# A fused DeltaNet and MLP kernel: another written-out order of its instructions behind entry 380

## The chip, the cores and the metric

The kernel runs on one core of a Trainium2 chip. The time is the device time of one execution in microseconds (us); the median of several executions counts. A profiled execution has a span as well, from its first to its last instruction. Five engines work beside each other, each through its own list of instructions in order: TensorE (PE, with its weight loads as PEld), VectorE (DVE), ScalarE (ACT), GpSimd (POOL) and SyncE (SP), which only issues transfers. ACT and POOL can issue transfers too.

## The reference

The first half is a delta rule over time, for 4 batches x 8 heads, 768 steps and a head size of 48, from a state of zeros (k_n is k divided by its norm plus 1e-6):

```python
for t in range(S):
    y[:, :, t] = np.einsum('bhd,bhde->bhe', q[:, :, t], state)
    v_old = np.einsum('bhde,bhd->bhe', state, kt)
    state = state + bt[:, :, :, None] * np.einsum('bhd,bhe->bhde', kt, vt - v_old)
```

The second half takes the 3072 rows of y (8 heads x 48 = 384 wide) through a two-layer network with a tanh GELU: `h = x @ w_in` (384 to 2048), `g = gelu(h)`, `out = g @ w_out` (2048 to 384). Inputs and output are float32.

## The kernel before

Time is cut into 12 chunks of 64 steps. A chunk c has two units, u = 2c and 2c + 1, of 16 (batch, head) pairs each, two of them stacked on the 128 partitions. All matmuls take bf16.

For a unit, `prep` (L470) makes bf16 copies of k and q and a scaled k (`kc`, `kb`, `qb`), turns them on their side (a transposing transfer `turn` on SP for most units), multiplies them into two masked 64x64 matrices per head (`G2` to `ln` and `G` to `wp`, both masked on DVE, L534), and then inverts a triangular 64x64 matrix per head in five rounds. Round i is a relay between engines: 8 matmuls `Ai` on PE (L575), an addition `rti` on DVE (L587; the tile is rt in rounds 1 to 3 and rl in rounds 4 and 5), 8 matmuls `Bi` on PE, and an eviction of the result from PSUM into the block-diagonal tile bd, from which the next round reads. Round 1 begins with `X1`, which fills bd from ln, mostly on POOL.

The eviction has three forms, and the order picks one for each unit and round. `bde` copies the two 64x512 halves apart (L332). `bdf` copies the lower half apart and brings the upper one as a 128x512 product with a column of zeros and ones (L338). `xi` copies all of it densely as one 128x512 (L332), after which two copies `bdc` (L617) spread it from SBUF into bd, on POOL or DVE.

For a chunk, `chain` (L620) carries the state on: `K` (state times keys), `R` on DVE (L660), `U` (the inverse times R, L670), its eviction `Un`, the state's growth `S` and `Sn` on DVE (L689), and the output of the chunk, `Q` and `O` (L647, L695), evicted by `On` and turned by `X` or by a transfer `turnx`. `mlp` (L716) then runs 48 matmuls of 128x256 in 16 groups `up` (L724), four GELUs on ACT (L728), 32 matmuls of 128x384 in 8 groups `down` (L735), evictions `Z0`, `Z1` and the transfers `out`.

What runs when is no loop: the string ORDER names every operation once, with the engine behind a colon where there is a choice and the PSUM bank behind an @. `order` (L154) makes the lists of the engines from it, and `emit` (L192) adds the waits that the data and the banks need. So an engine never passes a waiting instruction, and a transfer issued from ACT stands in ACT's list between its evictions. Two ways through a step (`A`, `rt` or `J`, `C`, `rj`; `nsq` or `nsa`) are picked by naming one of them.

```python
                for waits, o in plan[ename]:
                    for n, v in waits.items():
                        e.wait_ge(sems[n], v)
                    ins = o.fn(e, tile)
```

Of the kernel before, what the change touches and what calls it, by code (L numbers as in the profile page):

```python
# [16 lines left out]
ORDER = """  # L17
beta01:a one pad1 k0x1.11:a k0x0.01:a bdz0:g upone1 wz:d fill23@0 fill20@1 fill46@0 fill16@1 fill63@4 fill26@1 half:d fill25@0 fill12@2
fill54@5 ident pad3:g k0x0.10 tmplz:d tmpl0 k0x1.00:a k0x1.10:a k0x1.01:a mmup:d pad0 mmlo:d mlo0 fill64@0 k0x0.00 mlo1 tmpl1 two:d triln1:d
triwpm3:d triwpm1:d ladj16:d fill37@1 identf k0x0.11 ident2 ladj32:d fill28@4 sq.0a:d fill65@3 mup0 k1.00 fill56@4 sum.0a triln0:d fill41@1  # L20
fill52@6 beta00 betaT0@3 betaN000 betaN001 betaN010 betaN011 k1.01 epsb k1.10:a fill45@2 beta11:a k1.11 fill22@1 beta10 sq.0b:g tabS pow.0a
eps.0a twob:d J1.1@3 sum.0b q0.1 mup1 nsa.0a v0.11 inv.0a ib.0a upone0 v0.10 pow.0b fill55@2 q0.0:a eps.0b nsa.0b sq.1:d fill36@0 kb.0 kc.1
bdz1:g k2.10 fill49@2 inv.0b ib.0b:g kb.1:g betaT1@0 kc.0 Tc.1@1 fill9@2 betaA111 betaA110 betaA101 sum.1 pow.1 eps.1:g nsq.1:g kTc.1 q1.1
fill60@4 Tb.0@2 kTb.0 Tc.0@4 kTc.0 Tb.1@1 inv.1 triwpm0:d betaA100 ib.1 GM.0@6 ln.0 kb.3:g v1.11:a v0.01 X11.0 wpm.0 kTb.1:a GM.1@4 ln.1
X10.0 v0.00:a qb.0:a Tq.0@1 wpm.1 kc.3 Tk.3@2 triln3 A1.0@0 X10.1:d kTq.0 GQ.0@4 k2.00:a kTk.3:a q1.0:a X11.1 C1.1 rj1.1 rt1.0 B1.0@0 k2.01
pad2 kb.2 wpq.0 bde10.0 kc.2:d GM.3@6 ln.3 B1.1@1 bde10.1:d bde11.0 A2.0@0 rt2.0 bde11.1 A2.1@1 rt2.1 Tk.2@3 triwpm2 B2.0@2 B2.1@0 qb.1:a
v1.00 Tq.1@1 v1.10 v1.01 wpm.3 bde21.0:d k2.11 sq.2 sum.2 bde20.0 A3.0@2 fill1@4 fill4@5 fill42@4 fill14@5 q2.0 bdf20.1 bdf21.1:d A3.1@0
rt3.0 B3.0@2 kTk.2:a GM.2@4 rt3.1 triln2 ln.2 w2.1 qb.2:a bdz4:g bdz3:g X10.3 kTq.1:a X11.3 w1.1 A1.3@0 pad5:g pow.2 B3.1@1 k3.10 GQ.1@6
wpm.2 rt1.3 kc.5 k4.10 q2.1 bdf30.0 bdf31.0 A4.0@2 rt4.0 vs.1 B1.3@0 R0b.0:g bdf30.1 bdf31.1 A4.1@1 bdz2:g wpq.1 v2.00 bdf10.3 qb.3:g
eps.2:g B4.0@2 bde41.0 nsq.2:g bde40.0 X11.2 rt4.1 q3.0 X10.2 A1.2@4 rt1.2 B4.1@1 bde41.1:d w1.0 bde40.1 Tq.2@3 kTq.2 B1.2@4 bde10.2  # L30
triwpm4:g A5.0@5 rt5.0 A5.1@1 rt5.1 bde11.2 bdf11.3:d k3.01 B5.0@2 bde50.0 A2.2@3 rt2.2 B5.1@4 bde50.1:d bde51.0 k3.00 bde51.1 B2.2@0
bde21.2 bde20.2 inv.2 A2.3@1 rt2.3 R0a.0:g U.0@4 Un.0:d B2.3@1 A3.2@0 rt3.2 q4.0 Tq.3@2 O.0@4 On.0:d fill6@3 bde21.3 qb.5:g B3.2@0 bde20.3
A3.3@1 rt3.3 kTq.3:a GQ.3@6 X.0@2 xT.0:d B3.3@1 triwpm5:g bdf30.2 bdf31.2 A4.2@0 rt4.2 bdf30.3 bdf31.3:d up4.0@2 up12.0@4 up13.0 k3.11 wpq.3
ib.2:g kb.5:g B4.2@0 up5.0 up6.0 up7.0 up14.0 A4.3@1 up15.0 up0.0@6 q3.1 tabG bde41.2:d bde40.2 up1.0 up2.0 A5.2@0 rt4.3 gelu1.0 pad4:g
kb.4:g kc.7 up3.0 B4.3@1 w2.0 kc.4:g sq.3:g sum.3 k4.00 k5.10 q4.1 gelu3.0 gelu0.0 qb.4:g T.4@2 kT.4:a T.5@4 rt5.2 bde41.3:d bde40.3:d kT.5
pow.3 eps.3:g up8.0@6 up9.0 v2.11 A5.3@0 rt5.3 k5.00:a G2.5@2 ln.5 bdz5:g kc.6:g X11.5 k4.01:a G2.4@4 S.0@0 Sn.0 ln.4 X11.4 X10.4 G.4@2 wp.4
up10.0 qb.9:a up11.0 gelu2.0 nsq.3:g qb.6:g qb.7:g k4.11 K.1@0 R.1 inv.3 ib.3:g kb.6:g kb.7:g v3.11 G.5@4 wp.5 B5.2@2 sq.4 down10.0@3 A1.4@1
down00.0@0 bde51.2 rt1.4 kc.8 down01.0 X10.5 sum.4 pow.4 eps.4:g B5.3@4 bdf50.3 B1.4@1 bde10.4 k5.01 bde11.4:d down11.0 A1.5@5 rt1.5
down02.0 k5.11 sq.5:g kc.10:g A2.4@1 v4.10 v4.11 rt2.4 turn.7 v2.10 bdf51.3 bde50.2 B1.5@4 bde10.5:d bde11.5 down03.0 Z0.0 B2.4@2 v3.10
bde21.4:d kc.9:g U.1@6 Un.1 A2.5@5 rt2.5 q5.0 down12.0 GQ.2@0 wpq.2 Q.1@6 bde20.4 A3.4@2 turn.6 v3.00:a rt3.4 G2.7@4 O.1 On.1 S.1@0 Sn.1  # L40
nsq.4:g down13.0 inv.4 ib.4:g X.1@2 B2.5@6 xT.1:d kb.9:g v4.01 sum.5 pow.5 eps.5:g kb.8:g Z1.0 bde20.5 B3.4@7 bdf30.4 turn.9 fill47@3 v3.01
ln.7 bdf31.4 v2.01:a up0.1@0 up1.1 up2.1 up3.1 bde21.5:d gelu0.1 q6.1 A4.4@2 rt4.4 qb.8:a up8.1@4 up9.1 k7.00 A3.5@3 rt3.5 B4.4@2 bde41.4
k7.11 G2.6@0 ln.6 G.7@6 wp.7 q7.0 up10.1 B3.5@3 bde31.5 bde30.5 X10.6 up11.1 gelu2.1 up4.1@0 up5.1 up6.1 G.6@6 bde40.4:d A4.5@3 k6.10:a
up7.1 down10.1@2 wp.6 k7.10 rt4.5 A5.4@4 rt5.4 up12.1@6 out11.0 gelu1.1 X11.6 A1.6@5 X11.7 X10.7 A1.7@3 rt1.7 rt1.6 k7.01 turn.8 B4.5@4
bdf40.5 q6.0 up13.1 B5.4@0 up14.1 xi5.4:d bdf41.5 B1.7@3 bdf10.7 bdc50.4 up15.1 B1.6@1 bdc51.4 bde10.6:d bde11.6 out00.0 vs.2 A5.5@5
down11.1 down12.1 q7.1 rt5.5 bdf11.7:d B5.5@5 nsa.5 gelu3.1 xi5.5 bdc50.5 A2.6@4 rt2.6 sq.7 Q.2@0 K.2@6 R.2 bdc51.5 A2.7@3 rt2.7 k6.00:a
B2.6@4 xi2.6:d bdc21.6 down00.1@5 U.2@6 Un.2 down01.1 B2.7@3 inv.5 sum.7 bde20.7:d fill27@4 O.2 bdc20.6 q5.1 G2.8@6 ln.8 A3.6@4 X10.8 ib.5:g
bde21.7 A3.7@3 rt3.7 On.2 X11.8 turnx.2 v4.00:a down13.1 Z1.1 rt3.6 G.8@6 wp.8 k6.01 vs.3 k6.11 B3.7@0 bde31.7 bde30.7 S.2@2 Sn.2 kb.10:g
B3.6@4 kb.11:g down02.1 bde30.6 A1.8@6 rt1.8 down03.1 bde31.6 kc.11:g qb.11:g Z0.1 out00.1 out11.1 A4.7@0 rt4.7 A4.6@2 B1.8@3 bdf10.8
bdf11.8 G.9@4 G2.9@6 ln.9 up4.2@0 up5.2 up6.2 B4.7@3 up7.2 up0.2@6 up1.2 up2.2 k8.10:a wp.9 rt4.6 up8.2@4 B4.6@2 bde41.6:d X11.9 bdf40.7  # L50
bdf41.7 gelu1.2 up9.2 up10.2 up11.2 up3.2 A2.8@3 qb.12:a up12.2@0 bde40.6:d A5.6@2 qb.10:g rt5.6 gelu2.2 gelu0.2 up13.2 A5.7@4 rt5.7 up14.2
rt2.8 B5.6@2 xi5.6 X10.9 A1.9@5 rt1.9 pow.7 sq.6:g B5.7@4 xi5.7 turn.10 sum.6 bdc50.7 up15.2 gelu3.2 down00.2@3 B2.8@2 bde21.8 bde20.8:d
k8.01 B1.9@4 bde10.9 K.3@6 R.3 G2.10@0 down10.2@5 q8.1 q8.0 turn.11 A3.8@2 rt3.8 kc.13:g eps.7:g bdc50.6 bdc51.6 down01.2 bdc51.7 U.3@6
ln.10 X10.10:d X11.10 bde11.9 A2.9@2 B3.8@4 Q.3@0 rt2.9 v5.00 Un.3 O.3 On.3 turnx.3 G.10@6 pow.6 eps.6:g B2.9@2 bdf20.9 bdf21.9 bde30.8:d
down11.2 down02.2 down03.2 Z0.2 wp.10 A1.10@6 v6.11 rt1.10 A3.9@1 rt3.9 kc.12 qb.13:g k8.00 bde31.8 down12.2 k8.11 qb.15:a nsq.6:g inv.6
ib.6:g S.3@2 kb.12:g turn.12 Sn.3 down13.2 Z1.2 kb.13:g nsa.7 A4.8@0 B3.9@1 bdf30.9 rt4.8 G2.11@6 ln.11 G.11@2 wp.11 B4.8@0 bde40.8:d
# [742 lines left out]
```

## Time and profile before

| | |
|---|---|
| time, median of 3 runs | 264.47 us (260.86 to 264.93) |
| span of the profiled execution | 258.8 us |
| the profiled execution's own time | not given apart; the nearest of the three runs, 260.86 us, is 2.1 us over the span |
| PE busy | 242.1 us, 94% of the span |
| DVE busy | 209.5 us, 81% |
| ACT busy | 185.1 us, 72% |
| POOL busy | 136.2 us, 53% |

A busy share says that an instruction was in flight, from its issue to its result. For PE, whose matmuls overlap, it hides short stops between two matmuls; for the others it is nearer to the time that the instructions take. What bounds a stretch is read from the stretch. Entry 380 of the order, where the change begins, is reached at 47.6 us of the span or a little later.

### The profile page before, as it was taken

The page shows a single profiled execution, that of the slowest core. Times are in us where ns is not written, and L with a number is a line of the kernel's source. Part 1 is how long each engine was busy: PE and PEld are TensorE (multiplying, and loading weights), DVE is VectorE, ACT ScalarE, POOL GpSimd, SP SyncE. Part 2 cuts the span into 40 slices and gives each one's busy share as a digit, 9 for nine tenths or more (in the row PEclk, how much of TensorE's full clock was granted, in tenths as well). Part 3 has the DMA queues.
Part 4 walks back from the last instruction along what each step waited for, and adds up shares of the span by engine and source line. Part 5 has one row for each costly group of instructions (what it writes and reads, how often), then busy time and mean ns, then how long its engine had stood idle before and what let it go on. Part 6 is the DMA issues. An engine that isn't in the chain of part 4 may idle for free.

```text
span 258.8 us, 12244 instructions
## 1 busy us (share of the span) xinstructions
PE 242.1 (94%) x5490; PEld 189.6 (73%) x5490; DVE 209.5 (81%) x358; ACT 185.1 (72%) x295; POOL 136.2 (53%) x198
## 2 busy tenths in 40 slices
...
GB/s 88 200 191 182 212 185 200 135 132 151 164 198 146 167 107 134 159 102 165 160 47 157 155 96 185 53 74 123 155 66 106 128 48 4 3 5 124 30 63 61
DMA packets 116788, 31.46 MB, mean 122 GB/s; under 512 B 110848, under 2 KB 115968, under 8 KB 116736
## 3 DMA queue, kind: packets, MB, share of 16 engines
...
q8 instruction: 43, 0.70, 1.1%
...
## 4 chain that ended last, share of the span: by engine, by line
PE 81%; DVE 8%; POOL 4%; issue 3%; ACTq 2%; ACT 1%; POOLq 0%
PE ps L724 24%; PE ps L735 24%; PE ps L575 20%; PE ps L530 4%; PE ps L647 3%; PE ps L670 2%; PE ps L695 2%; ACTq L432 2%; DVE rt L587 1%; PE ps L682 1%; DVE wp L534 1%; POOL nrm L458 1%; DVE ln L534 1%; PE ps L394 1%; POOL bd L564 1%
## 5 line engine op out<-in xcount | busy, mean ns | idle before, releaser
L332 ACT ACTIVATE bd<-ps 64x512 bf16<-64x512 f32 x127 | 72.8, 587 | 20.5 <-PE ps L575 18.7
L724 PE MATMUL ps<-xT,W 128*128 128x256 bf16 x576 | 76.3, 273 | 0.7 <-issue 0.7
L735 PE MATMUL ps<-W,gT 128*128 128x384 bf16 x384 | 73.8, 326 | 0.0
L728 ACT ACTIVATE gT<-ps 128x1024 bf16<-128x1024 f32 x48 | 48.5, 1020 | 15.1 <-PE ps L724 14.7
L724 PEld LDWEIGHTS ps<-xT,W 128*128 128x128 bf16 x576 | 50.7, 98 | 7.2 <-issue 1.0
L587 DVE TENSOR_TENSOR rt<-ps,two 128x512 bf16<-128x512 f32 x71 | 47.6, 683 | 5.4 <-PE ps L575 4.9
L735 PEld LDWEIGHTS ps<-W,gT 128*128 128x128 bf16 x384 | 33.0, 97 | 16.9 <-ACT gT L728 0.2
L564 POOL TENSOR_SCALAR_AFFINE_SELECT bd<-ln 64x512 bf16<-64x512 bf16 x44 | 29.1, 664 | 24.5 <-DVE ln L534 20.9
L332 DVE CAST bd<-ps 64x512 bf16<-64x512 f32 x51 | 34.8, 686 | 5.2 <-PE ps L575 4.2
L534 DVE CAST_PREDICATED wp<-mup,ps 128x1024 bf16<-128x1024 uint16 (+1 forms) x28 | 29.7, 1062 | 1.5 <-PE ps L530 1.4
L575 PE MATMUL ps<-rt,bd 128*128 128x64 bf16 x576 | 28.5, 195 | 2.0 <-DVE rt L587 1.5
L458 POOL TENSOR_TENSOR nrm<-nrm,half 128x16 f32<-128x16 f32 x9 | 26.2, 2908 | 7.6 <-DVE nrm L456 7.4
L617 POOL COPY bd<-xi 64x256 f32<-64x256 f32 x27 | 10.8, 404 | 34.6 <-DVE xi L332 19.5
L575 PE MATMUL ps<-wp,bd 128*128 128x64 bf16 (+1 forms) x576 | 27.1, 189 | 1.5 <-POOL bd L564 1.0
L575 PEld LDWEIGHTS ps<-rt,bd 128*128 128x128 bf16 x576 | 23.5, 99 | 6.7 <-DVE rt L587 2.4
L575 PEld LDWEIGHTS ps<-wp,bd 128*128 128x128 bf16 x576 | 23.0, 98 | 6.2 <-POOL bd L564 1.5
L587 DVE TENSOR_TENSOR rl<-ps,two 128x384 bf16<-128x384 f32 (+1 forms) x48 | 23.0, 484 | 4.8 <-PE ps L575 4.4
L575 PE MATMUL ps<-ln,bd 128*128 128x48 bf16 (+1 forms) x384 | 18.8, 190 | 2.8 <-issue 1.6
L575 PE MATMUL ps<-rl,bd 128*128 128x64 bf16 x384 | 18.8, 193 | 0.7 <-DVE rl L587 0.7
L575 PEld LDWEIGHTS ps<-ln,bd 128*128 128x128 bf16 x384 | 15.5, 98 | 5.2 <-issue 1.8
L575 PEld LDWEIGHTS ps<-rl,bd 128*128 128x128 bf16 x384 | 15.7, 98 | 3.0 <-DVE rl L587 1.1
L485 POOL TENSOR_TENSOR tok<-kraw,nrm 128x384 bf16<-128x384 f32 x19 | 15.6, 829 | 4.2 <-PE ps L682 2.7
...
## 6 DMA issues: line engine op xcount, KB each, us to landing
qraw<-in_q_dram SPq DMA_DIRECT2D x21, 192.0 KB, 5.0
out_dram<-ob SPq DMA_DIRECT2D x21, 192.0 KB, 3.4
...
W<-in_moe_w_in_dram POOLq DMA_DIRECT2D x2, 768.0 KB, 10.1
...
```

The source lines that it names most:

```text
L332: return e.activation(out, in_, ACT.Copy) if e is nc.scalar else e.tensor_copy(out, in_)
L458: if e is nc.scalar else e.tensor_tensor(nr[:, 1, hx], nr[:, 0, hx], half[:, hx], ALU.pow), reads=[nrn, "half"] + ["one", "roots"] * (c < ...
L485: A(("dve", "pool"), op("kb"), lambda e, P: e.tensor_tensor(kb, kr, nr[:, 5, hx].unsqueeze(2).to_broadcast(full), ALU.mult), reads=[f"kraw ...
L530: ins = e.matmul(o, kT[s][r, y, g, hf(a)], src)
L534: return e.copy_predicated(out.rearrange("p (x g) t -> p x g t", x=2), mask[:, 0:wd].bitcast(U16).unsqueeze(1).unsqueeze(1).to_broadcast([ ...
L564: A(("pool", "dve"), op(f"X1{a}"), lambda e, P, src=ln[m][hf(a), :, :], dst=bd[b_][hf(a), :, hf(a)], a=a: e.affine_select(out=dst, in_=src ...
L575: ins = e.matmul(P(name)[:, C * h + cs.start:C * h + cs.stop], bd[b_][:, h, :], rhs[:, h, cs], **kw)
L587: A(("dve",), op(f"rt{i}"), lambda e, P, i=i, cs=cs, cn=cn, r_=r_: e.tensor_tensor(r_[:, :, cs], P(ps(f"A{i}")).rearrange("p (h t) -> p h ...
L617: A(("pool", "dve"), op(f"bdc{i}{a}"), lambda e, P, src=xi[i_][hf(a), :, :], dst=bd[b_][hf(a), :, hf(a)]: e.tensor_copy(dst.bitcast(F32), ...
L724: ins = e.matmul(P(ph)[:, 256 * f:256 * f + 256].rearrange("p (x t) -> p x t", x=2), W1[:, j, 128 * (i + f):128 * (i + f) + 128], x_[:, :, ...
L728: A(("act",), f"gelu{i // 4}.{c}", lambda e, P, i=i, ph=ph: e.activation(g_[:, i:i + 4, :], P(ph).rearrange("p (f t) -> p f t", f=4), ACT. ...
L735: ins = e.matmul(P(po)[:, 0:DM], g_[:, f, 128 * b:128 * b + 128], W2[:, f, :], start=(f == 0), stop=(f == FC - 1))
```

## The change

Only the string ORDER is replaced, and with it the file is 7 lines shorter: a line L332 of before is L325 of after, and so on. The first 380 entries name the same operations on the same engines. Behind them the order is new throughout; a line of it on each side:

```diff
-up10.0 qb.9:a up11.0 gelu2.0 nsq.3:g qb.6:g qb.7:g k4.11 K.1@0 R.1 inv.3 ib.3:g kb.6:g kb.7:g v3.11 G.5@4 wp.5 B5.2@2 sq.4 down10.0@3 A1.4@1
...
-rt2.8 B5.6@2 xi5.6 X10.9 A1.9@5 rt1.9 pow.7 sq.6:g B5.7@4 xi5.7 turn.10 sum.6 bdc50.7 up15.2 gelu3.2 down00.2@3 B2.8@2 bde21.8 bde20.8:d
...
+X10.4:g G.4@2 wp.4 up10.0 qb.9:a up11.0 gelu2.0 nsq.3:g qb.6:g qb.7:g k4.11:s K.1@0 X10.5:g v2.10:s G.5@4 down00.0@2 B5.3@3 wp.5 A1.4@6 bde51.3:a inv.3
...
+up6.2 bdf41.7:a A5.7@1 up7.2 bdc11.8:g qb.15:a A5.6@0 gelu2.2 up3.2 bdc10.8:g X10.9:g sum.6 X11.9:g rt5.7 out00.1:a out11.0:a A2.8@5 B5.7@1 rt5.6 A1.9@0
```

In a few words the change is given as: first 380 entries of the order kept, another new order behind them, with 35 dense evictions, late transfers and GpSimd's hold on VectorE in the plan. Counted from the two strings, behind entry 380:

| | before | after |
|---|---|---|
| operations on PE | 572 | 573 (`A2.5` becomes `J2.5` and `C2.5`) |
| operations on DVE | 260 | 265 |
| operations on ACT | 230 | 230 |
| operations on POOL | 137 | 145 |
| transfers issued by ACT, by SP | 18, 111 | 47, 82 |
| dense evictions `xi` on ACT, on DVE | 11, 5 | 20, 9 |
| halves evicted apart (`bde` and `bdf`) on ACT, on DVE | 120, 52 | 114, 32 |
| spreading copies `bdc` on POOL, on DVE | 27, 5 | 45, 13 |
| other work of DVE that reads SBUF alone (`X1`, `kb`, `kc`, `qb`, `sq`, `vs`) | 7 | 16 |

Three places, named as the profile names them; what stands in front of an arrow is written.

On PE, from `U.3` (rs1 with bd0 and bd1) to `O.3` (us1 with wp0 and wp1), which reads what ACT's `Un.3` makes of `U.3`. Before:

```order
L670 MATMUL ps<-rs1,bd0 128x48 x8
L670 MATMUL ps<-rs1,bd1 128x48 x8
L575 MATMUL ps<-ln1,bd3 128x64 x8
L575 MATMUL ps<-rt0,bd2 128x64 x8
L647 MATMUL ps<-st1,kT0 64x48 x32
L695 MATMUL ps<-us1,wp0 64x48 x16
L695 MATMUL ps<-us1,wp1 64x48 x16
```

After, the same stretch:

```order
L663 MATMUL ps<-rs1,bd0 128x48 x8
L663 MATMUL ps<-rs1,bd1 128x48 x8
L728 MATMUL ps<-W20,gT2 128x384 x4
L568 MATMUL ps<-ln1,bd3 128x64 x8
L640 MATMUL ps<-st1,kT0 64x48 x32
L523 MATMUL ps<-kT0 64x128 x16
L688 MATMUL ps<-us1,wp0 64x48 x16
L688 MATMUL ps<-us1,wp1 64x48 x16
```

A group `down` of the MLP (L728) and the products `G.10` (L523) have come between, and 8 matmuls on rt0 have gone behind.

On ACT, around the GELUs of chunk 2 (gT2; ob is the output tile, kraw the keys as loaded). Before:

```order
L332 ACTIVATE bd2<-ps 64x8x64
L338 ACTIVATE bd2<-ps,up10 128x8x64
L432 DMA kraw2<-in_k_dram 64x8x48
L332 ACTIVATE bd1<-ps 64x8x64
L338 ACTIVATE bd1<-ps,up10 128x8x64
L728 ACTIVATE gT2<-ps 128x1024
L332 ACTIVATE tok0<-qraw0 128x8x48
L728 ACTIVATE gT2<-ps 128x1024 x2
L332 ACTIVATE xi0<-ps 128x512
L332 ACTIVATE xi1<-ps 128x512
L728 ACTIVATE gT2<-ps 128x1024
```

After:

```order
L325 ACTIVATE xi2<-ps 128x512
L740 DMA out_0_dram<-ob0 64x2x384
L331 ACTIVATE bd1<-ps,up10 128x8x64
L325 ACTIVATE tok0<-qraw1 128x8x48
L721 ACTIVATE gT2<-ps 128x1024
L740 DMA out_0_dram<-ob1 64x2x384
L740 DMA out_0_dram<-ob0 64x2x384
L721 ACTIVATE gT2<-ps 128x1024
L425 DMA kraw2<-in_k_dram 64x8x48
L721 ACTIVATE gT2<-ps 128x1024
```

The load of keys has moved in among the GELUs, and three transfers of the output, which SP issued before, stand beside it in ACT's list.

On DVE, the last 12 instructions up to the mask of unit 14 (ln2). Before:

```order
L332 CAST bd5<-ps 64x8x64
L460 TENSOR_SCALAR nrm8<-nrm8 128x16
L338 TENSOR_SCALAR bd5<-ps,up10 128x8x64
L587 TENSOR_TENSOR rt0<-ps,two0 128x512
L587 TENSOR_TENSOR rl1_0<-ps,two0 128x8x32 x2
L466 RECIPROCAL nrm8<-nrm8 128x16
L332 CAST bd4<-ps 64x8x64
L332 CAST xi2<-ps 128x512
L332 CAST bd0<-ps 64x8x64
L587 TENSOR_TENSOR rt1<-ps,two0 128x512
L587 TENSOR_TENSOR rt0<-ps,two0 128x512
L534 COPY_PREDICATED ln2<-mlo0,ps 128x512
```

After:

```order
L580 TENSOR_TENSOR rt1<-ps,two0 128x512
L580 TENSOR_TENSOR rt0<-ps,two0 128x512
L325 CAST bd1<-ps 64x8x64
L455 TENSOR_TENSOR nrm8<-nrm8 128x16
L580 TENSOR_TENSOR rl1_0<-ps,two0 128x8x32
L459 RECIPROCAL nrm8<-nrm8 128x16
L448 TENSOR_TENSOR sq1<-kraw0 128x768
L610 COPY bd0<-xi0 64x8x32
L460 TENSOR_TENSOR nrm8<-nrm8,bsb0 128x16
L580 TENSOR_TENSOR rt1<-ps,two0 128x512
L580 TENSOR_TENSOR rt0<-ps,two0 128x512
L527 COPY_PREDICATED ln2<-mlo0,ps 128x512
```

Five evictions from PSUM have become one, and a spreading copy (L610), a square of the keys (L448) and a further step on their norms (L460) have come in.

More of the change, by code (lines that the diff above doesn't have):

```diff
@@ L15 @@
 ENGINES = {"p": "pe", "a": "act", "d": "dve", "g": "pool", "s": "sp"}
[L17 to L20, printed above, removed]
@@ L41 @@
[L41 to L44, printed above, removed]
```

171 lines of the change are left out of this document (86 added, 85 removed).

## The prediction

> **What bounds the kernel now.** I read the page first, then the stretches, the chain of waits and what PE's weight loads waited for. The page:
>
> ```profile
> PE 242.1 (94%) x5490; PEld 189.6 (73%) x5490; DVE 209.5 (81%) x358; ACT 185.1 (72%) x295; POOL 136.2 (53%) x198
> ```
>
> By stretch (from:to, length, then busy us and instructions of PE, PEld, DVE, ACT, POOL, then granted clock, DMA share, GB/s):
>
> ```profile
> 0.00:47.60 47.60, 38.33 (x775) 28.10 (x775) 42.68 (x98) 34.69 (x64) 31.30 (x57) 0.93 1.16 180
> 47.60:80.00 32.40, 30.94 (x803) 23.23 (x802) 29.68 (x45) 24.14 (x40) 23.28 (x35) 1.00 1.06 159
> 80.00:120.00 40.00, 39.46 (x1003) 31.88 (x1001) 34.61 (x54) 31.61 (x51) 33.46 (x46) 1.00 0.79 133
> 120.00:140.00 20.00, 20.00 (x472) 16.34 (x470) 19.26 (x32) 17.29 (x29) 9.80 (x12) 1.00 0.70 130
> 140.00:180.00 40.00, 38.72 (x949) 31.33 (x948) 34.10 (x55) 30.53 (x49) 20.51 (x28) 1.00 0.67 110
> 180.00:240.00 60.00, 59.28 (x1397) 47.99 (x1394) 48.62 (x78) 39.64 (x60) 17.86 (x24) 1.00 0.40 74
> 240.00:258.80 18.80, 15.38 (x113) 10.69 (x110) 0.56 (x1) 7.17 (x9) 0.00 (x0) 1.00 0.22 53
> ```
>
> The first row holds the 380 entries that stay, and with them all of the reduced clock and 9.3 of the 16.7 us in which PE was idle. Behind it PE is idle for 7.4 us, 3.4 of these in the last row, after its last matmul. DVE comes next: 166.3 of the 192.4 us from 47.6 to 240, and 19.26 of 20 between 120 and 140. ACT has 143.2 in the same 192.4 us. So PE bounds this part, with DVE close beside it for a while.
>
> The chain shows what PE's work costs when nothing holds it (start, us, what):
>
> ```profile
> 60.90 0.68 issue
> ...
> 68.48 0.70 PE ps L575 x24
> ...
> 72.83 0.63 PE ps L647 x64
> ...
> 173.90 0.89 issue
> ...
> 244.94 5.24 PE ps L724 x48
> 250.18 5.21 PE ps L735 x32
> 255.42 0.49 ACT ob L332
> ```
>
> That is 109 ns for a matmul of `up`, 163 for one of `down`, 29 for one of the inversion and 10 for one of the small ones. At the end the MLP of the last chunks runs for over 10 us without a gap; no order shortens that.
>
> What a gain can come from is what stops PE. Its weight loads, from 47.6 us on (waiter, releaser: us in total, times, longest):
>
> ```profile
> PEld ps L575 <- issue: 2.5, 4, 1.0
> PEld ps L530 <- issue: 2.1, 7, 0.5
> PEld ps L724 <- issue: 1.0, 1, 1.0
> PEld ps L695 <- issue: 0.8, 2, 0.5
> PEld ps L575 <- POOL bd L564: 0.7, 1, 0.7
> ...
> PEld ps L670 <- POOL bd L617: 0.3, 1, 0.3
> ...
> PEld ps L575 <- DVE rl L587: 0.2, 1, 0.2
> ```
>
> The answer has 26 rows. Five are "issue", 6.6 us together, for which the profile shows no one who is waited for; I leave them as they are. The other 21, from the 0.7 down to the 0.2 of the last one, sum to 6.4 us. **So 6.4 us, 2.4% of the time, is all that an order can visibly win behind entry 380.**
>
> **The change part by part.** *TensorE's neighbours.* Where one of those waits arises, in before (start, us, engine):
>
> ```profile
> 93.09 0.56 PE L670 MATMUL ps<-rs,bd 128*128 128x48 bf16 x16
> ...
> 93.69 0.81 ACT L332 ACTIVATE us<-ps 128x768 bf16<-128x768 f32 x1 [0.60 <-PE ps L670]
> ...
> 94.05 0.44 PE L647 MATMUL ps<-st,kT 48*64 48x48 bf16 x32
> ...
> 94.67 0.44 PE L695 MATMUL ps<-us,wp 64*64 64x48 bf16 x32 [0.18 <-PE ps L647]
> ```
>
> `Un.3` begins when `U.3` is through (93.65) and ends at 94.50; `O.3` starts at 94.67. Between them PE has 16 matmuls at 29 ns and 32 at 10, 0.78 us, to cover from the issue of U's last matmul to 94.67, about 1.15 us (16 x 29 ns after 93.09 is 93.55). After, the first fence on PE has 4 x 163 + 8 x 29 + 32 x 10 = 1.20 us there, and 16 matmuls `G.10` on top. So this wait goes. Not all do: around `O.11` the order of PE's neighbours is as it was. And the new order has as many relays as the old one, each able to wait. Bounds: nothing won (every wait that goes is replaced), and 6.4 us (all go). I take a third, 2.0 us: nearer to nothing, since 21 waits among some 570 operations are the rest that a written order leaves, and a new order leaves a rest too.
>
> *The other path of unit 5.* `J2.5` adds one matmul of 512 columns, by the 163 ns for 384 columns 0.22 us on PE, and takes an addition from DVE; a wash.
>
> *The evictions.* Durations (busy, mean ns behind the bar):
>
> ```profile
> L332 ACT ACTIVATE bd<-ps 64x512 bf16<-64x512 f32 x127 | 72.8, 587 | 20.5 <-PE ps L575 18.7
> ...
> L332 DVE CAST bd<-ps 64x512 bf16<-64x512 f32 x51 | 34.8, 686 | 5.2 <-PE ps L575 4.2
> ...
> L617 POOL COPY bd<-xi 64x256 f32<-64x256 f32 x27 | 10.8, 404 | 34.6 <-DVE xi L332 19.5 <-ACT xi L332 14.0
> ...
> L338 ACT ACTIVATE bd<-ps,up 128x512 bf16<-128x512 f32 x19 | 12.8, 672 | 0.5 <-DVE bd L332 0.5
> ...
> L338 DVE TENSOR_SCALAR bd<-ps,up 128x512 bf16<-128x512 f32 x11 | 8.2, 742 | 2.2 <-ACT bd L332 2.2
> ...
> L332 ACT ACTIVATE xi<-ps 128x512 bf16<-128x512 f32 x11 | 6.3, 593 | 1.1 <-PE ps L575 1.0
> ...
> L332 DVE CAST xi<-ps 128x512 bf16<-128x512 f32 x5 | 3.4, 685 | 0.2 <-PE ps L575 0.2
> ...
> L332 DVE CAST us<-ps 128x768 bf16<-128x768 f32 x2 | 1.9, 954 | 0.7 <-PE ps L670 0.7
> ...
> L617 DVE COPY bd<-xi 64x256 f32<-64x256 f32 x5 | 1.4, 286 | 0.8 <-ACT xi L332 0.7
> ```
>
> DVE loses 16 halves at 0.686 and 4 scaled ones at 0.742, 13.9 us. It gains 4 dense evictions (2.7), 8 spreading copies (2.3), 2 `Un` (1.9), a square and 2 `vs` of 768 elements (no row has them on DVE; by the 0.954 of the same width 2.9), and 6 pieces of 384 to 512 elements (`X1`, `kc`, `qb`: between 0.286 and 0.685, taken at 0.4: 2.4). That is 12.2, net **-1.7 us** of 166. Only the fuller stretches feel it, 47.6 to 80 and 120 to 140, so it is under 0.5 us of time and lies inside the third above.
>
> ACT trades 27 plain halves for 10 plain and 11 scaled ones (-15.8 + 5.9 + 7.4), gains 9 dense ones (+5.3) and gives up 2 `Un`: about +1 us of 143, in its idle time. POOL gains 18 copies, 7.3 us, and gives up about as much in other work.
>
> What a dense eviction costs is latency: 0.593 and two copies of 0.404, 1.40 us, where two halves on ACT take 1.17. With 13 more that is 3.0 us if PE had nothing else; its cover is the other units and the MLP between `Bi` and the next `A`. The POOL row of the waits above bounds it: 27 copies in 16 dense evictions made PE wait for 0.3 us in all. I take 13/16 of it, 0.2 us.
>
> *The transfers.* 29 more are issued by ACT (start, us, engine; ACTq is the issue):
>
> ```profile
> 102.47 1.02 ACT L728 ACTIVATE gT<-ps 128x1024 bf16<-128x1024 f32 x1 [0.22 <-PE ps L724]
> 102.71 0.60 ACTq L432 DMA_DIRECT2D vraw<-in_v_dram  x1
> 103.52 0.59 ACT L332 ACTIVATE bd<-ps 64x512 bf16<-64x512 f32 x1
> ```
>
> The issue takes 0.60 us, while the GELU ahead of it still runs, and the eviction behind it starts 0.03 us after the GELU's end. At that price 29 cost 0.9 us of ACT, off the path; without cover they cost 29 x 0.60 = 17.4 us of ACT. I take 0. SP loses the same 29, from 111, and its transposes `turn` stand behind fewer loads.
>
> "Late" is not late for PE. A load lands in some microseconds (KB each, median us):
>
> ```profile
> qraw<-in_q_dram SPq DMA_DIRECT2D x21, 192.0 KB, 5.0
> ```
>
> At the prices above, the written orders put, for chunks 5 to 11, at least 26 us of PE work between the last load of a chunk's keys and the first matmul on them before, and 30 after; for the queries 16 and 17. That is cover several times over, for the work on POOL and DVE between as well. I take 0; one load that came 5 us late would cost up to 5 us, since PE passes nothing.
>
> Sum: -2.0 + 0.2 (dense) + 0.2 (J) and DVE's share of -0.4: **-2.0 us**. The profiled span becomes 256.8 us. Its own time isn't given; the nearest run is 260.86, 2.1 over the span. The median, 264.47, is 3.6 above that run, about what the first row's clock (7% of 47.6, 3.3 us) would cost once more: an estimate, the runs don't show their clock. That part of the order is unchanged, so I take the 2.0 off the median: 262.5 us.
>
> **The rivals.** *Nothing moves* (264.5): each wait that goes comes back elsewhere. For it speaks that PE streams 94% of the time already.
>
> *VectorE is held by GpSimd.* The words of the change have this hold in the plan, yet the new order has more of what could suffer: DVE's work within SBUF, spreading copies included, goes from 12 pieces to 29. In before:
>
> ```profile
> L485 DVE TENSOR_TENSOR tok<-kraw,nrm x5: 551/558/855, 9.7 to 165.2; 128x384 bf16<-128x384 f32 x5
> ```
>
> The same instruction took 855 ns once and 558 mostly. At 0.30 us each the 17 more cost DVE 5.1 us; half of that on the path gives 262.5 + 2.6 = 265.1, all of it 267.6. The Trainium skill (SBUF — State Buffer, Who interferes with whom) says that a VectorE instruction with two SBUF inputs, or in a two-port mode, and a GpSimd instruction lock each other out for a whole instruction, which would let a wait be as long as GpSimd's longest; this trace shows no more than the 0.30 us.
>
> *ACT pays for the transfers* (slower). Its place is ACT's list wherever the instruction ahead of a transfer is shorter than 0.60 us or two transfers follow each other, as behind the second GELU in the fence on ACT: 1.20 us of issue against 1.02 us of cover, and a GELU behind it on which `down` waits. It decides from about half of the issue time uncovered and waited for: 29 x 0.30 = 8.7 us, 271.2. Against it: the row above, and 49 us of idle ACT. The Trainium skill (DMA: Bandwidth & Descriptors, Issuing engines are not separate DMA queues) says that all queues end on the same 16 DMA engines, so that another issuing engine saves no more than the sequencer's time; by that the move buys nothing that could pay for this. No row here shows that a second queue moves data faster.
>
> *All visible waits go* (faster): 264.5 - 6.4 = 258.1. For it speaks that place on PE, where the new spacing covers the whole relay; against it, that no order so far is without a rest.
>
> **How the numbers follow.** What a measurement of this kernel tells from no change is about 2%, 5.3 us. Chances: the forecast 0.42 (262.5), nothing moves 0.17 (264.5), the hold 0.11 (265.1 to 267.6), ACT 0.12 (271.2), all waits gone 0.18 (258.1). So faster 0.18, same 0.70, slower 0.12. The range leaves out ACT's case and the far end of the fast one: 257.5 to 268.5. It also holds the 3.6 us between the runs.
>
> **What would show it.** Right: PE's waits on other engines behind 47.6 us fall from 6.4 to about 4.4; "issue" stays near 6.6; DVE between 120 and 140 drops below 19; ACT's evictions behind a transfer start within 0.1 us. Wrong: gaps in ACT of 0.3 us and more behind transfers (ACT's rival); DVE pieces within SBUF that take 0.3 us longer than their shortest (the hold); PE rows that wait for POOL's bd L617 (by its line after, L610) with over 1 us; a new wait of PE on a transfer, which before has nowhere behind 47.6 us.

## The result and the profile after

Over 17 runs each the changed kernel takes 260.93 us (259.31 to 261.99), the kernel before 263.59 us (260.57 to 266.31). The ratio is 0.9942, with a 95% interval of 0.9916 to 0.9967: 0.9 to 2.2 us faster, 1.5 in the middle. The ratios here and below leave out single runs that were over 1.5% above the fastest of the same kernel; the medians keep them, and the profiles of b_shift210, a_plain, a_queues_before2, b_shift210_queues and a_evictions_before are of such runs.

The page of after, first its engines, then the instruction loads, which stand alike in before:

```profile
PE 242.8 (94%) x5491; PEld 190.4 (74%) x5491; DVE 209.1 (81%) x363; ACT 185.4 (72%) x295; POOL 137.7 (53%) x206
...
q8 instruction: 43, 0.70, 1.1%
```

The busy times are those of before within 1.5 us. The profiled execution took 259.31 us (span 257.6), the fastest of the 17, so one pair of profiles flatters the change; the experiments bring more of them. The stretches of after (columns as in the prediction):

```profile
47.60:80.00 32.40, 32.40 (x831) 25.30 (x830) 30.03 (x49) 27.68 (x45) 27.24 (x39) 1.00 0.97 149
80.00:120.00 40.00, 38.70 (x987) 31.82 (x986) 35.79 (x56) 31.34 (x52) 26.93 (x34) 1.00 0.81 138
120.00:140.00 20.00, 19.46 (x460) 15.63 (x458) 19.09 (x32) 15.35 (x25) 13.06 (x21) 1.00 0.89 163
140.00:180.00 40.00, 39.59 (x984) 32.05 (x981) 36.03 (x60) 30.40 (x47) 23.59 (x30) 1.00 0.57 106
180.00:240.00 60.00, 59.39 (x1375) 47.02 (x1372) 45.49 (x73) 39.21 (x58) 15.88 (x28) 1.00 0.37 68
```

TensorE gains between 47.6 and 80 (32.40 of 32.40 us, 30.94 before) and loses a little between 80 and 120. VectorE, which was to become lighter, has 166.4 us from 47.6 to 240, and 166.3 before.

What TensorE's weight loads waited for from 47.6 us on in after (waiter, releaser: us in total, times, longest):

```profile
PEld ps L568 <- issue: 1.8, 3, 1.2
PEld ps L640 <- issue: 1.4, 5, 0.3
PEld ps L523 <- issue: 1.2, 5, 0.3
PEld ps L568 <- DVE ob L325: 1.0, 1, 1.0
...
PEld ps L568 <- ACT bd L325: 0.2, 1, 0.2
```

Three rows of "issue" make 4.4 us, 6.6 before. The other 20 make 6.0 us, 6.4 before. So what the prediction took as fixed fell, and what it took the gain from hardly moved.

### What "issue" is

TensorE's timeline in before, at one of these stops (start, us, what, in brackets the idle time ahead):

```profile
173.70 0.20 PE L575 MATMUL ps<-ln,bd 128*128 128x48 bf16 x1
174.79 0.33 PE L575 MATMUL ps<-ln,bd 128*128 128x48 bf16 x7 [0.89 <-issue]
```

It cuts a group of eight equal products behind the first of them, and the profile names no one who is waited for. I numbered TensorE's records (products, weight loads and the few others) in order of time, 11,088 in before and 11,085 in after, and looked up the long stops. They have the same number modulo 256:

```
           number mod 256: start of the last product ahead, us over the stream
before     192: 60.6 0.85  76.6 0.53  107.6 0.53  147.6 0.56  190.5 0.85   191: 173.7 1.06
after      192: 92.6 1.27
```

The page's 43 instruction loads of 0.70 MB are 16 KB each, and 11,088 / 43 is 258: TensorE's program comes in pieces of 256 instructions. The trace has the start of each load. In before, behind 47.6 us, it begins 0.6 to 2.9 us after TensorE has come to the end of a piece, and takes 0.9 to 1.4 us. In the seven stops above TensorE goes on 1.3 to 1.6 us after the load of the next piece has ended. So from the end of one piece some 4 us pass on average before TensorE can go beyond the end of the next, and a piece that is run through in less can bring a stop: the one that ended at 173.7 took 2.2 us, since it holds mostly products of 8 to 29 ns. It need not: in after four pieces were run through in 2.9 to 3.5 us without a stop, and the loads that they needed had begun 0.1 to 0.7 us after the end ahead. The load for the stop at 92.6, behind a piece of 5.8 us, began 3.9 us late and took 1.8. On average a load begins 1.6 us late in before and 1.2 in after. The Trainium skill (Runtime: NRT & Kernel Launch, Instruction fetch mechanics) has the 16 KiB blocks of 256 instructions fetched while the current block runs, and the cost of an end of a block "mostly hidden"; the trace agrees on the size, and shows up to 1.3 us at one end that were not hidden.

### The profile page after: what moved, and what is told of

It reads as the page before. It is cut to its first block, busy times and chain, and to the rows that moved or that the text cites. A ratio compares the mean times of both kernels' runs of the same rounds, so it can differ in the third digit from the quotient of the medians.

```text
span 257.6 us, 12254 instructions
## 1 busy us (share of the span) xinstructions
PE 242.8 (94%) x5491; PEld 190.4 (74%) x5491; DVE 209.1 (81%) x363; ACT 185.4 (72%) x295; POOL 137.7 (53%) x206
## 4 chain that ended last, share of the span: by engine, by line
PE 82%; DVE 12%; ACTq 2%; ACT 2%; issue 1%
PE ps L728 24%; PE ps L717 24%; PE ps L568 21%; PE ps L523 4%; PE ps L640 3%; DVE bd L325 2%; DVE rt L580 2%; PE ps L663 2%; DVE wp L527 2%; ACTq L425 2%; DVE ln L527 2%; PE ps L688 1%; PE ps L675 1%; DVE kT L325 1%; PE ps L387 1%
## 5 line engine op out<-in xcount | busy, mean ns | idle before, releaser
L717 PE MATMUL ps<-xT,W 128*128 128x256 bf16 x576 | 77.6, 273 | 0.0
L325 ACT ACTIVATE bd<-ps 64x512 bf16<-64x512 f32 x110 | 62.8, 588 | 19.2 <-PE ps L568 17.8
L728 PE MATMUL ps<-W,gT 128*128 128x384 bf16 x384 | 74.2, 326 | 0.0
L728 PEld LDWEIGHTS ps<-W,gT 128*128 128x128 bf16 x384 | 33.2, 98 | 16.6 <-ACT gT L721 0.2
L610 POOL COPY bd<-xi 64x256 f32<-64x256 f32 x45 | 19.3, 429 | 46.9 <-ACT xi L325 25.7
L557 POOL TENSOR_SCALAR_AFFINE_SELECT bd<-ln 64x512 bf16<-64x512 bf16 x42 | 28.3, 674 | 14.9 <-DVE ln L527 10.2
L568 PE MATMUL ps<-wp,bd 128*128 128x64 bf16 (+1 forms) x576 | 28.3, 190 | 1.7 <-DVE ob L325 0.6
L325 DVE CAST bd<-ps 64x512 bf16<-64x512 f32 x35 | 23.8, 686 | 2.9 <-PE ps L568 2.2
L331 ACT ACTIVATE bd<-ps,up 128x512 bf16<-128x512 f32 x30 | 20.1, 675 | 0.9 <-DVE bd L325 0.7
```

Of the source, the lines that this page charges most:

```text
L325: return e.activation(out, in_, ACT.Copy) if e is nc.scalar else e.tensor_copy(out, in_)
L331: return e.activation(out, in_, ACT.Copy, scale=up1[:, 0:1]) if e is nc.scalar else e.tensor_scalar(out, in_, up1[:, 0:1], None, op0=ALU.mult)
L557: A(("pool", "dve"), op(f"X1{a}"), lambda e, P, src=ln[m][hf(a), :, :], dst=bd[b_][hf(a), :, hf(a)], a=a: e.affine_select(out=dst, in_=src ...
L568: ins = e.matmul(P(name)[:, C * h + cs.start:C * h + cs.stop], bd[b_][:, h, :], rhs[:, h, cs], **kw)
L610: A(("pool", "dve"), op(f"bdc{i}{a}"), lambda e, P, src=xi[i_][hf(a), :, :], dst=bd[b_][hf(a), :, hf(a)]: e.tensor_copy(dst.bitcast(F32), ...
L717: ins = e.matmul(P(ph)[:, 256 * f:256 * f + 256].rearrange("p (x t) -> p x t", x=2), W1[:, j, 128 * (i + f):128 * (i + f) + 128], x_[:, :, ...
```

## The experiments

All ratios are to the kernel before, run on the same chip beside them; its medians there were 262.9 to 264.8 us.

| label | what | median, us | ratio, 95% |
|---|---|---|---|
| b_shift210 | before, program shifted by 210 | 261.50 | 0.9898 (0.9846 to 0.9949) |
| b_shift216 | before, shifted by 216 | 262.17 | 0.9961 (0.9919 to 1.0004) |
| a_shift210 | after, shifted by 210 | 264.22 | 1.0032 (0.9996 to 1.0068) |
| a_shift256 | after, shifted by a whole piece | 262.17 | 0.9935 (0.9906 to 0.9964) |
| a_shift16 | after, shifted by 16 | 263.95 | 0.9963 (0.9920 to 1.0007) |
| a_shift210_light | a_shift210, less data to load | 263.34 | 0.9994 (0.9956 to 1.0031) |
| a_plain | after again | 262.20 | 0.9946 (0.9903 to 0.9989) |
| a_queues_before | after, transfers on before's engines | 264.38 | 0.9998 (0.9951 to 1.0044) |
| a_queues_before2 | the same kernel again | 262.09 | 0.9945 (0.9899 to 0.9991) |
| b_queues_after | before, transfers on after's engines | 273.88 | 1.0268 (1.0211 to 1.0326) |
| b_shift210_queues | both changes to before | 272.32 | 1.0314 (1.0249 to 1.0379) |
| a_evictions_before | after, 23 dense evictions taken back | 270.00 | 1.0238 (1.0170 to 1.0306) |

From the profile of each: the stops of over 0.12 us at ends of pieces, the waits of TensorE's weight loads on other engines, and the time from its first product of entry 380 or later to the start of its last, all from entry 380 on. A few of TensorE's records are missing from some traces, so an end is taken with eight instructions of tolerance. Two long stops are in both columns: 1.5 us in b_shift210, and 1.8 us in b_queues_after, where TensorE goes on 0.05 us after a GELU ends, so that it is a wait for ACT in part or whole.

```
                     stops   waits   time behind entry 380
before                4.5     6.2     207.1
a_shift210            4.5     6.1     208.6
a_shift210_light      3.4     6.3     207.5
after                 1.6     6.0     205.3
a_plain               0.9     6.8     206.7
a_shift256            2.0     7.1     207.6
a_queues_before       2.1     5.1     206.6
a_queues_before2      2.9     5.5     207.5
a_shift16             1.2     7.6     205.4
b_shift210            3.0     6.7     206.9
b_shift216            2.4     6.4     205.4
b_queues_after        4.6    16.5     215.7
b_shift210_queues     2.2    16.8     217.0
a_evictions_before    1.5    15.0     214.4
```

### Moving the ends of the pieces, not the order

```diff
+PIECES = {23: 8, 20: 8, 46: 8, 16: 8, 63: 8, 26: 8, 25: 8, 12: 8, 54: 8, 64: 8, 37: 8, 28: 8, 65: 8, 56: 8, 41: 8}
...
-                A(PE, n, lambda e, P, n=n: e.matmul(P(n), wz[:, 0:128], wz[:, :]), reads=["wz"], alloc=(n, 1), frees=[n], mode="m", mm=1)
+                A(PE, n, lambda e, P, n=n, w=512 // PIECES.get(i, 1): [e.matmul(P(n)[:, x:x + w], wz[:, 0:128], wz[:, x:x + w]) for x in range(0, 512, w)][-1],
+                  reads=["wz"], alloc=(n, 1), frees=[n], mode="m", mm=PIECES.get(i, 1))
```

> The kernel before, with its order word for word; only the first 15 warm-up products are each issued as 8 products of 64 columns instead of one of 512, so that TensorE's list has 210 instructions (105 products and their weight loads) more ahead of 12 us, for the same number of streamed columns. In the traces of before and after, the long stops of TensorE without a releaser stand at every 256th instruction of its list (number 192, 448, ...), and the page has 43 loads of instructions of 16 KB, as many as 11,088 instructions make in pieces of 256. Theory 1 (program loads): a stop comes where a piece is run through in less than about 4 us, before the next one has landed. Moved by 210 instructions, the pieces behind 47.6 us that are run through in under 4 us bring 1.0 us of stops instead of 3.9 in before; so the time falls by 2 to 3.3 us, from 263.6 to 260.3-261.6, and the stops at 60.6, 76.6, 107.6, 147.6, 173.7 and 190.5 us are gone from these places. Theory 2 (the one of the prediction: what the order makes engines wait for): the number of an instruction means nothing; the stops stay at these products, the time stays within 0.7 us of 263.6.

> The kernel after, with the same splitting of 15 warm-up products. Theory 1 (program loads): in this order the same shift puts the ends of the pieces at worse places: by the same sum 7.0 us of stops instead of 3.0, so 2 to 4 us slower than after, 263 to 265, with stops of 0.3 us and more at six or more ends of pieces behind 47.6 us. Theory 2 (the order's waits): within 0.7 us of 260.9.

> Control: the kernel after with 18 warm-up products in 8 pieces and two in 2, which adds 256 instructions, one whole piece, so that the ends of all later pieces stand where they stood. Theory 1: as after, 260.9 within 0.7 us. Theory 2: the same. If it is over 1 us away, the splitting itself changes the start of the kernel and the other two have to be read against it.

The same edit made before faster by 1.0% and after slower by 0.9% (1.0032 against 0.9942), and a shift by a whole piece left after where it was. Theory 2 has no place for the first two. TensorE's timeline in a_shift210:

```profile
94.28 0.37 PE L644 MATMUL ps<-st,kT 48*64 48x48 bf16 x22
95.51 0.27 PE L644 MATMUL ps<-st,kT 48*64 48x48 bf16 x10 [0.86 <-issue]
...
192.89 0.64 PE L527 MATMUL ps<-kT 48*64 48x128 bf16 x30
193.96 0.24 PE L527 MATMUL ps<-kT 48*64 48x128 bf16 x2 [0.44 <-issue]
```

Two runs of 32 equal products are cut, behind the 22nd and the 30th; after has no stop at either. With the stops of before (4.5 us in both), after's order is no faster than before's: 1.0032, interval 0.9996 to 1.0068. In b_shift210 the six places of before are free of stops, but 3.0 us stand at others, for 1.0 expected. The profile puts 1.5 of these, at 82.2, down to DVE; but TensorE goes on there 1.6 us after the load of the next piece has ended, as at the other stops. Its time behind entry 380 is only 0.2 us under that of before, so where its 1.0% lies is not seen in this one profile.

> A version meant to beat both: the kernel before, with its order, with 216 instructions more in TensorE's list (15 warm-up products in 8 pieces, one in 4). By the sum for program loads of 4 us this has the least stops of all shifts, 0.6 us behind 47.6 us (1.0 at 210, 3.9 in before, 3.0 in after). Program loads: 0.987 to 0.991 of before, so 0.3 to 0.7% below after. If the first result (0.9898) was chance: within 0.3% of before.

> The kernel after with one warm-up product in 8 pieces and one in 2, 16 instructions more in TensorE's list. By the same sum as for the shift by 210 (a program load takes about 4 us from the end of the piece before), the stops behind 47.6 us are 1.8 us instead of 3.0. Program loads: 0.3 to 1.2 us faster than after, ratio to before about 0.991. The order's waits alone: as after, 0.994.

These two missed: 0.9961 for 0.987 to 0.991, and 0.9963 for 0.991. The profiles have the stops low (2.4 and 1.2 us), but a fixed 4 us for each load is too coarse to rank shifts that differ by 1 us, and the intervals are as wide. No version is shown to beat after; b_shift210 (0.9898) lies below it, with overlapping intervals.

### Is it the data traffic?

```diff
-                        A(("sp", "act"), f"{n}{c}.{a}", lambda e, P, a=a, view=view: e.dma_start(raw["q"][s][hf(a), :, :], view[a, c]),
+                        A(("sp", "act"), f"{n}{c}.{a}", lambda e, P, a=a, view=view, h=16 if c < 6 else 2: e.dma_start(raw["q"][s][hf(a), 0:h, :], view[a, c][:, 0:h, :]),
-                    xs = slice(0, H) if x is None else slice(4 * x, 4 * x + 4)
+                    xs = (slice(0, H) if c < 6 else slice(0, 1)) if x is None else slice(4 * x, 4 * x + 4)
```

> The kernel after, shifted by 210 instructions (which was slower: 1.0032), with the loads of k, q and v from chunk 6 on cut to one of eight heads: the other heads of these chunks are computed from old data, so the output is left wrong for them; every wait and instruction stays, only the data traffic behind some 50 us falls. If the program loads are late because they stand behind data traffic: the delay from the end of a piece to the start of the next load falls from 1.1 us on average to below 0.5, the stops of 0.4 to 1.0 us at six ends of pieces behind 70 us go, and TensorE's time from entry 380 to its last product falls from 208.6 us by 2 to 4. If a program load takes its time whatever the traffic: the stops stay at these places and the time falls by under 1 us.

Five of the seven stops stayed at their places, two (at 77.5 and 134.0 in a_shift210) went. TensorE's timeline in a_shift210_light, where a_shift210 has 0.44:

```profile
192.78 0.64 PE L527 MATMUL ps<-kT 48*64 48x128 bf16 x30
194.42 0.24 PE L527 MATMUL ps<-kT 48*64 48x128 bf16 x2 [1.00 <-issue]
```

The DMA share between 120 and 140 fell from 0.94 to 0.53, the mean delay before a load only from 1.2 to 1.0 us, the stops from 4.5 to 3.4 and the time behind entry 380 by 1.1. So a load of the program takes some 3.5 us (1.0 for the delay, 1.1 for the load, 1.4 until TensorE goes on) with less traffic too; single stops became longer and others shorter.

### The transfers on ACT

```diff
-... v4.01:a ... v3.10:a ... k7.11:a ...
+... v4.01:s ... v3.10:s ... k7.11:s ...
```

> The kernel after, in its order, but each of the 49 transfers that changed their issuing engine is issued from the engine that issued it in before (39 back from ACT to SP, 10 back from SP to ACT). If ACT pays for its transfers: faster than after, by up to 8.7 us. If they are free, as predicted: 260.9 within 0.7 us. Third: in the traces the delay between the end of a piece of TensorE's program and the start of the next load of instructions is shorter in after; if the emptier SP queue does that, the delays grow here again and the time rises by 1 to 3 us.

> The kernel after with the transfers on before's engines, once more: the first time its interval (0.9951 to 1.0044) touched that of after (0.9916 to 0.9967), and its profile showed no wait that would explain 1.5 us, except 0.5 us on one transposing transfer. If the issuing engine matters in this order: 0.4% or more above the unchanged kernel after beside it. If it doesn't (the prediction's zero): within 0.2% of it.

> The kernel after, unchanged, beside the others of this call on one chip, and a second profile of it. Ratio to before 0.994 again. If TensorE's stops at the ends of program pieces are what its time behind entry 380 goes with, this second profile has its own sum of them, and the time from entry 380 to the last product is 205.3 us plus or minus the difference in these stops (1.4 us in the first profile); the waits on other engines stay at 6 to 7 us. If the first profile's gain was the order's waits, they are again below before's 6.2 to 6.4.

The first time, handing the transfers back looked like a cost (0.9998), the second shows none: 0.9945 against 0.9946. In the order of after it does not matter to the time by more than the half per cent that these runs resolve. The third possibility fails too: the mean delay of a program load, 1.2 us in after, is 1.2 to 1.3 in these two. a_plain missed its forecast: with 0.7 us less of stops it should have taken less time behind entry 380 than after's first profile, and took 1.4 us more. How ACT in after takes its transfers (ACTq is the issue):

```profile
84.74 1.01 ACT L721 ACTIVATE gT<-ps 128x1024 bf16<-128x1024 f32 x1
85.19 0.79 ACTq L740 DMA_DIRECT2D out_dram<-ob  x1
86.02 1.02 ACT L721 ACTIVATE gT<-ps 128x1024 bf16<-128x1024 f32 x1 [0.28 <-PE ps L568]
86.05 1.12 ACTq L425 DMA_DIRECT2D kraw<-in_k_dram  x1
87.21 1.02 ACT L721 ACTIVATE gT<-ps 128x1024 bf16<-128x1024 f32 x1 [0.17 <-PE ps L568]
```

The issues begin beside the activation ahead, but some outlast it, and the next activation begins 0.04 to 0.05 us after the issue's end. So ACT stood still for at most 0.28 and 0.17 us here, and 0.61 at 150.58 behind the second of two issues in a row, though the profile names PE each time. That is more than the 0.1 us that the prediction allowed. In this profile TensorE does not stop behind it. In a_plain, the same kernel, it does (ACT and PE):

```profile
89.15 0.52 ACT L325 ACTIVATE tok<-qraw 128x384 bf16<-128x384 f32 x1 [2.22 <-DMA qraw<-in_q_dram]
...
89.58 1.01 ACT L721 ACTIVATE gT<-ps 128x1024 bf16<-128x1024 f32 x1
89.82 1.41 ACTq L740 DMA_DIRECT2D out_dram<-ob  x1
90.73 0.39 PE L568 MATMUL ps<-ln,bd 128*128 128x64 bf16 x8 [1.15 <-ACT gT L721]
...
91.27 1.03 ACT L721 ACTIVATE gT<-ps 128x1024 bf16<-128x1024 f32 x1 [0.69 <-PE ps L568]
...
92.35 0.50 PE L717 MATMUL ps<-xT,W 128*128 128x256 bf16 x3 [0.53 <-ACT gT L721]
```

ACT waits 2.22 us for a load of queries, so the GELU behind it is late and TensorE stands 1.15 us; then an issue of 1.41 us outlasts that GELU, the next one is late too, and TensorE stands 0.53 us. a_shift256 has the same two waits with 1.14 and 0.35 us. ACT's wait for that load is there in all five profiles of after's order with its own queues and full data (0.76 to 2.22 us), and in neither profile with before's queues.

> The kernel before, in its order, but each of the 49 transfers that changed their issuing engine is issued from the engine that issues it in after (39 from ACT instead of SP, 10 from SP instead of ACT). The other way round, in the order of after, these queues were worth some 0.6% (ratio to before 0.9998 with the queues of before, 0.9935 and 0.9942 with its own). If the queues alone bring that (transfers issued later, so less traffic ahead of a program load or of a load that is waited for): faster than before by 1 to 2 us, 262 to 262.5. If it takes after's order with them, or the difference came from something else: within 0.7 us of 263.6. If ACT pays for them (the rival of the prediction): over 1 us slower.

> The kernel before with both: 15 warm-up products in 8 pieces each (210 instructions more in TensorE's list, which alone gave 0.9898) and the 49 transfers on the engines of after. If the queues work through the program loads: there are few stops left to remove, so 0.990 as with the shift alone, 261. If they work in another way: 0.983 to 0.986, 259.3 to 260.

In the order of before the same engines cost 7 us, as the third possibility for b_queues_after had it; with the shift on top (1.0314) neither possibility for b_shift210_queues came true, and the shift that had brought 1.0% brought nothing here. TensorE's waits in b_queues_after, from 48 us on:

```profile
PEld ps L575 <- ACT bd L332: 5.1, 6, 1.8
PEld ps L575 <- ACT bd L338: 2.0, 1, 2.0
PEld ps L647 <- ACT gT L728: 1.9, 2, 1.7
```

and ACT's timeline at the 2.0:

```profile
86.12 0.49 ACT L332 ACTIVATE ob<-ps 128x384 f32<-128x384 f32 x1
86.64 2.17 ACTq L747 DMA_DIRECT2D out_dram<-ob  x2
88.85 0.59 ACT L332 ACTIVATE bd<-ps 64x512 bf16<-64x512 f32 x1 [2.24 <-PE ps L724]
```

Two transfers of the output stand behind each other and ahead of two evictions that TensorE waits for; the two issues take 2.17 us, not 2 x 0.60. That no activation runs beside them does not explain it: at the start of before ACT issues six loads in 4.05 us, 0.68 each, with none beside them. Why some issues close behind another take longer was not traced. The profile names PE as what ended ACT's idle time, but the eviction begins 0.04 us after the second issue. That is the prediction's rival of ACT, with its place, and it costs 7 us where the rival priced 8.7; only the order is another one.

### The dense evictions

```diff
-... sq.5:a xi3.4:a kb.9:g ... xT.1:d bdc30.4:g ... up1.1 v3.10:a bdc31.4:g up2.1
+... sq.5:a bdf30.4 bdf31.4 kb.9:g ... xT.1:d ... up1.1 v3.10:a up2.1
```

> The kernel after with the 23 dense evictions that only it has taken back: each xi and its two spreading copies become the two evictions (bde or bdf) that before has for this unit and round, on before's engines, at the place of xi. DVE gets 18 evictions for 7 dense ones and some 9 copies, about 5 us more work; ACT 28 for 16, about 7 us more; POOL 37 copies less. If a dense eviction costs 0.2 us in all, as predicted, and the relief of DVE and ACT is worth under 0.5: within 0.7 us of after. If the dense ones are what makes after faster (DVE and ACT free in time for TensorE): 1 to 3 us slower, with more waits of TensorE on DVE and ACT. If their latency (1.40 us against 1.17) is on the path: up to 2 us faster.

0.9946 became 1.0238, 7.7 us more, far beyond the 1 to 3 of the strongest expectation. TensorE's waits, from 48 us on:

```profile
PEld ps L568 <- ACT bd L331: 2.6, 4, 1.0
...
PEld ps L568 <- DVE rt L580: 1.6, 2, 1.4
```

All waits on other engines are 15.0 us instead of 6 to 7. The new places of TensorE's work count on ACT and DVE being free, and the dense forms make them free. It does not say that dense evictions would help before's order, where the pairs have places of their own, nor how much of the 7.7 us is DVE's work and how much ACT's.

## Why the prediction was right, and where it was not

**The number.** 262.5 was forecast from a median of 264.47, and -2.0 us. Over 17 runs it is 1.5 less (0.9 to 2.2), and the median 260.93 lies in the range. The sign and the size came out for a reason that the prediction had set aside, so that the size fits is luck. Its sum also takes DVE's share twice: it "lies inside the third above", and is then subtracted as another 0.4.

**TensorE's neighbours, "a third" of 6.4 us: the step that failed.** The wait at `O.3` went, in a_plain as worked out; in after's first profile the stop of 1.27 us at 92.6 lies inside that stretch and hides it. But the waits of the weight loads on other engines are 6.0 us in after's first profile and 6.8 in its second, with before's 6.2 counted the same way from entry 380. New ones took the place of the old. And these 6.4 us were never all TensorE's time, since weight loads run beside products. What the products themselves waited for, from entry 380 on, in before and then in after:

```profile
PE ps L575 <- POOL bd L564: 0.4, 1, 0.4
...
PE ps L695 <- PE ps L647: 0.2, 1, 0.2
```

```profile
PE ps L568 <- DVE ob L325: 0.6, 1, 0.6
PE ps L523 <- DVE wp L527: 0.5, 1, 0.5
PE ps L568 <- DVE bd L325: 0.4, 1, 0.4
PE ps L523 <- ACT bd L325: 0.2, 1, 0.2
```

So of the 6.4 us only some 0.5 (0.54 before rounding) show as stops of the products, in a list that has those over 0.15 us, and in after these rose: to 1.7 us, and 3.2 in a_plain. The upper two of after stand in both its profiles. That is the rival "nothing moves", for these waits, and the end of the other one, "all visible waits go".

**"Issue", 6.6 us, "I leave them as they are": the term that carried it.** At before's ends of pieces the stops are 4.5 us in its one profile, at after's 0.9 to 2.9 in five, 1.9 on average: 2.6 us less. Not only the place of the ends did it: after has short pieces too, but the loads begin earlier, and why they do is not shown. Some of the 2.6 us is given back: the stops of the products on other engines, 0.5 us in before, are 1.1 to 3.2 in seven profiles of after's order (a_shift210_light and a_evictions_before left out). In the five profiles with after's ends the time behind entry 380 is 205.3 to 207.6 us, 206.7 on average, against 207.1 in the one of before, so the profiles show less than the 1.5 us of the runs. That the ends of the pieces are worth time is shown by the shifts of after, and less surely by those of before; that they are the whole of the 1.5 us is suggested by a_shift210, which has before's sum of stops and before's time, not more.

**The evictions and DVE's -1.7 us.** DVE lost the 13.9 us as counted (30.0 to 19.0 for the halves, 5.9 to 3.0 for the scaled ones), but the six pieces of "384 to 512 elements", taken at 2.4 us, cost 4.8 (`X1` went from 1.2 to 3.2, the casts of q from 0 to 2.0, those of k from 0.3 to 1.1). By shapes, from 47.6 us on in after:

```profile
L559 DVE TENSOR_TENSOR bd<-ln,twob 64x512 bf16<-64x512 bf16 x5 | 3.2, 631 | 0.1
...
L325 DVE CAST tok<-qraw 128x384 bf16<-128x384 f32 x2 | 2.0, 1006 | 0.0
```

DVE between 120 and 140 is 19.09, not below 19. The 0.2 for a dense eviction's latency was right as far as TensorE's waits show it: none on POOL's copies (L610) in after, and 0.3 us on one of DVE's. That the relief was "under 0.5 us" does not hold for this order: with the dense forms taken back it loses 7.7 us.

**The transfers, 0:** right in the time of after within what these runs resolve, though ACT pays up to 0.7 us for some and TensorE 0.53 us for one in a_plain, behind a GELU of the very fence that the rival named; and wrong in the order of before, since the price is the place in ACT's list. **Late loads, 0:** right for TensorE's own operands in after, where it waits for no transfer behind 47.6 us. But the load of queries that ACT waits for reaches it through the GELU, with 1.15 us in a_plain and 1.14 in a_shift256; the prediction's cover counted TensorE's work, and not what stands behind the load in ACT's list. **`J2.5`:** not told apart by any run.

**VectorE held by GpSimd: the mechanism is there, with far more than 0.30 us for a held piece, and few pieces held.** In after (DVE, POOL and PE):

```profile
118.16 0.41 DVE L559 TENSOR_TENSOR bd<-ln,twob 64x512 bf16<-64x512 bf16 x1
...
128.57 0.85 POOL L610 COPY bd<-xi 64x256 f32<-64x256 f32 x2
129.11 1.50 DVE L559 TENSOR_TENSOR bd<-ln,twob 64x512 bf16<-64x512 bf16 x1
129.38 0.50 POOL L325 CAST tok<-kraw 128x384 bf16<-128x384 f32 x1
129.83 0.50 POOL L325 CAST tok<-qraw 128x384 bf16<-128x384 f32 x1
...
130.53 1.21 DVE L527 CAST_PREDICATED wp<-mup,ps 128x1024 bf16<-128x1024 uint16 x1
...
131.79 0.42 PE L523 MATMUL ps<-kT 48*64 48x128 bf16 x16 [0.53 <-DVE wp L527]
...
152.83 1.47 POOL L448 TENSOR_TENSOR sq<-kraw 128x768 f32<-128x768 f32 x1
152.85 1.67 DVE L325 CAST tok<-qraw 128x384 bf16<-128x384 f32 x1
```

`X1` (L559) takes 0.41 us when nothing holds it, the cast of q 0.34 (at 168.06). The cast at 152.85 began 0.02 us after a square of 1.47 us on POOL and ended 0.22 after it: held for nearly the whole of it, 1.33 us. `X1` lost 1.09 us beside a row of short ones, and so `wp` is late, on which TensorE then waits. The Trainium skill (SBUF — State Buffer, Who interferes with whom) says that whichever of the two engines issues first holds the ports that they share for its whole instruction; the cast's 1.33 of 1.47 us agrees with that. These two pieces cost DVE 2.4 us, where the rival priced 5.1 for seventeen; most such pieces were not held, so it stayed a part of what was given back.

**The 3.6 us between runs, put down to the clock: not borne out.** Beside the first experiments before took 262.15 us in one run and 265.01 in another, at granted clocks of 0.980 and 0.981. And the second profile of after is 4.0 us longer than the first, 2.6 of these up to entry 380. That stretch in the second profile, then in the first:

```profile
0.00:51.10 51.10, 38.11 (x807) 27.74 (x811) 43.47 (x98) 35.43 (x65) 31.56 (x57) 0.97 1.09 173
```

```profile
0.00:48.50 48.50, 40.07 (x807) 29.34 (x811) 43.53 (x98) 35.34 (x65) 31.96 (x57) 0.89 1.15 180
```

The longer one has the higher clock (0.97 against 0.89). What it waited for is in the timeline of that second profile:

```profile
43.48 1.46 POOL L448 TENSOR_TENSOR sq<-kraw 128x768 f32<-128x768 f32 x1 [5.47 <-DMA kraw<-in_k_dram]
...
45.45 1.24 PE L487 MATMUL ps<-ident,tok 128*128 128x128 bf16 x19 [1.84 <-POOL tok L325]
```

A load of keys comes 3.3 us later than in the first (where POOL's square begins at 40.15), and TensorE stands 1.84 us behind it, in the part that both kernels share. Over all profiles entry 380 is reached between 48.0 and 53.7 us. Why that load is sometimes late was not tried.
